# Windowed attention ahead of two MoE layers: q and k with one token to a partition, v's second copy made on the chip, zero fills moved, last output halves reordered

## The chip, the cores and the metric

The kernel runs on one core of one Trainium2 chip. The metric is the device time of one execution in microseconds; a table below gives the median of three runs and the one execution that was profiled. Engines are named as in the profile: PE is TensorE, PEld its weight loads, ACT is ScalarE, DVE is VectorE, POOL is GpSimd, SP is SyncE, which issues all transfers here.

## What is computed

An attention over 2 batches, 8 heads, 576 tokens and 64 columns a head, in which each query sees 32 keys: heads 0 to 3 the last 32 tokens, heads 4 to 7 every fourth token of the last 128. Its output, 1152 tokens by 512 columns, goes through a layer of 2048 columns with the Mish function and then through four experts of 1024 columns whose outputs are summed by probability.

```python
def _attn_ref(q, k, v):                      # q, k, v: [2, 8, 576, 64]
    scores = (1 / np.sqrt(D)) * np.matmul(q, k.transpose(0, 1, 3, 2))
    mask_plain = (rel >= 0) & (rel < 32)
    mask_dil = (rel >= 0) & (rel < 128) & (rel % 4 == 0)
    scores = np.where(masks, scores, -1e9)   # heads 0-3 plain, 4-7 dilated
    attn = np.exp(scores - max); attn = attn / (sum + 1e-09)
    return np.matmul(attn, v)

h = x @ w_in;  g = h * np.tanh(softplus(h));  x = g @ w_out
for e in range(4):
    out += p[:, e:e + 1] * (np.maximum(x @ w1[e], 0) @ w2[e])
```

`w_in` and `w_out` arrive as 64-bit floats.

## The kernel before

The program is scheduled by hand: each engine runs its instructions in the order of the source, and an engine waits where an operand of another engine or of a transfer is not there yet. Two accesses of one PSUM bank by different engines are put in order too.

**Attention units.** The attention is cut into ten units, five chunks of 128 tokens (the fifth of 64) for each of two batches (`Unit`, from L292). A unit's life is spread over several steps of `att_step` (L436). In step s the unit s+5 has its q and k loaded, s+2 is transposed on TensorE (`transposes`, L320), s+1 is copied from PSUM to SBUF on ScalarE (`spread`, L338), s has its scores (L344 to L355), its max, subtract and exp (`softmax`, L363 to L365) and the transposes of its probabilities (`probsT`, L377), s-1 has these copied (`probsT_copy`, L382) and multiplied by v (`values`, L389 and L393), its sums (L369) and its normalising (`normalise`, L401), and s-2 is transposed (`xT`, L409) and written as a high and a low part (`x_hi`, L420, ScalarE; `x_lo`, L424, VectorE).

**q and k.** A tile `nat` holds pairs of tokens: k on partitions 0 to 63 and q on 64 to 127, 128 columns (two tokens of one head) for each head, loaded in runs of 512 bytes, q and k each onto 64 partitions (L311). Eight transposes lead to PSUM, and eight ScalarE copies (L338) sort parity and head into `qkP` (heads 0 to 3) and `qkD` (heads 4 to 7), in which the two heads of a pair stand block by block in a matrix whose other blocks are zero. These zeros are written once by memsets (`zero_k`), for the first chunk on VectorE and for the rest on GpSimd.

**v.** `vP` and `vD` hold for each query block the keys of the block before (32 partitions) and its own (32 partitions), so that each token of v is there twice. Both copies are loaded from DRAM (L265, L269, L284, L288), in runs of 256 bytes for `vP` and of 1024 for `vD`. The zero blocks are GpSimd memsets at the start (`zero_v`).

**Weights.** `w_in` and `w_out` come as 32 blocks of 512 KiB onto 128 partitions into three buffers `raw` (`dec_load`, L131 and L134). Each is decoded over three steps: VectorE shifts (L150) and merges (L157), ScalarE makes a 16-bit rounding (L173) and the high part (L179), GpSimd the low part (L164). In the attention one block a step passes through; `dec_dve` stands at the end of a step, `dec_act` in its middle. Three blocks are loaded ahead, in steps -1, 0 and 1; after that each freed buffer is filled again.

**After the attention.** The first layer's multiplies (`first`, L497, and `second`, L517) begin in the last two steps of the attention; then follow the two layers' multiplies (L497, L517, L700, L753). At the end each tile of 128 rows of the output is multiplied by its probability on VectorE (`finish`, L767) and stored (L769); the last tile is cut into two halves of 256 columns that lie in one PSUM bank.

Of the kernel before, what the change touches and what calls it, by code (L numbers as in the profile page):

```python
# [8 lines left out]
F32 = mybir.dt.float32  # L9
# [14 lines left out]
def kernel(  # L24
# [177 lines left out]
    def zero_v(c):  # L202
        blk = slice(4 * c, min(4 * c + 4, S // 32))
        for j in range(2):
            POOL.memset(vP[64 * j:64 * j + 64, :, blk, 1 - j, :], 0.0)
            if c == 0:
                POOL.memset(vP[64 * j:64 * j + 32, :, 0, j, :], 0.0)
        if c in (0, NCH - 1):
            POOL.memset(vD[:, :, :, c], 0.0)
        else:  # L210
            for j in range(2):
                POOL.memset(vD[64 * j:64 * j + 64, :, 1 - j, c], 0.0)

    def zero_k(c, eng):
        n = min(128, S - 128 * c)
        for j in range(2):
            rows = slice(64 * j, 64 * j + 64)
            eng.memset(qkP[rows, :, 1 - j, 32 + 128 * c:32 + 128 * c + n], 0.0)
            eng.memset(qkD[rows, :, 1 - j, c + 1, :, 0:n // 2], 0.0)
# [15 lines left out]
    DVE.memset(qkP[:, :, 0:2, 0:32], 0.0)  # L235
    for p in range(2):
        DVE.memset(qkD[:, p, 0:2, 0], 0.0)
        DVE.memset(qkD[:, p, 0:2, NCH, :, (S % 128) // 2:64], 0.0)
    zero_k(0, DVE)
# [20 lines left out]
    def load_vP(b, g0, g1):  # L260

        for j in range(2):
            src = v[b, j:j + 1]
            if g0 == 0:
                SP.dma_start(out=vP[64 * j + 32:64 * j + 64, :, 0, j, :],  # L265
                             in_=bass.AP(src.tensor, src.offset, [[D, 32], [2 * S * D, 2], [1, D]]))
            g = max(g0, 1)
            for p in range(2):
                SP.dma_start(out=vP[64 * j:64 * j + 64, p, g:g1, j, :],  # L269
                             in_=bass.AP(src.tensor, src.offset + (2 * p * S + 32 * (g - 1)) * D,  # L270
                                         [[D, 64], [32 * D, g1 - g], [1, D]]))

    def load_vD(b, c0, c1):

        for j in range(2):
            src = v[b, 4 + j:5 + j]
            lo, n = 64 * j, 64
            off = src.offset + 128 * (c0 - 1) * D
            if c0 == 0:
                lo, n, off = lo + 32, 32, src.offset  # L280
            elif c1 == NCH:
                n = 32 + (S - 128 * c0) // 4
            if c1 == c0 + 1:
                SP.dma_start(out=vD[lo:lo + n, :, j, c0, :],  # L284
                             in_=bass.AP(src.tensor, off, [[4 * D, n], [2 * S * D, 2], [1, 4 * D]]))
                continue
            for p in range(2):
                SP.dma_start(out=vD[lo:lo + n, p, j, c0:c1, :],  # L288
                             in_=bass.AP(src.tensor, off + 2 * p * S * D,
                                         [[4 * D, n], [128 * D, c1 - c0], [1, 4 * D]]))  # L290


    v_loads = {-2: [(load_vD, 0, 1, NCH - 1)], -1: [(load_vP, 0, 8, S // 32), (load_vD, 0, NCH - 1, NCH)],
               2: [(load_vD, 1, 0, 1), (load_vP, 1, 0, 8)], 4: [(load_vD, 1, 1, NCH - 1)],
               5: [(load_vP, 1, 8, S // 32), (load_vD, 1, NCH - 1, NCH)]}

    class Unit:
# [8 lines left out]
        def load_qk(self):  # L306

            self.nat = ap1.tile([128, H, 2 * D], F32, tag="nat", name=nm("nat"), bufs=4)
            rows = slice(128 * self.c, 128 * self.c + self.n)
            for lo, src in ((0, k), (self.n // 2, q)):  # L310
                SP.dma_start(out=self.nat[lo:lo + self.n // 2],  # L311
                             in_=src[self.b, :, rows, :].rearrange("h (t two) d -> t h (two d)", two=2))

        def transposes(self):
            n = self.n
            self.pts = []
            for g in range(2):
                pt = bank(self.tbanks[g]).rearrange("p (h t) -> p h t", h=4)
                for h in range(4):
                    PE.transpose(pt[:, h, 0:n], self.nat[0:n, 4 * g + h, :], ident[0:n, 0:n])  # L320
                self.pts.append(pt[:, :, 0:n].rearrange("p (a j) (k t) -> p a j k t", j=2, k=2))

        def spread(self):

            n, c = self.n, self.c

            def move(g, par, j):
                src = slice(64 * par, 64 * par + 64)
                dst = slice(64 * j, 64 * j + 64)
                if g == 0:  # L330
                    cols = 32 + 128 * c
# [104 lines left out]
    def att_step(s, mid=None, pre=None):  # L436
# [3 lines left out]
        if n1:  # L440
            n1.spread()
# [473 lines left out]
```

## Time and profile before

| what | us |
|---|---|
| median of 3 runs | 666.11 (664.84 to 666.72) |
| the profiled execution | 663.83 |
| its span from the first to the last instruction | 662.1 |
| TensorE busy | 637.3 (96%) |
| VectorE, ScalarE, GpSimd busy | 290.9, 274.9, 158.4 |

The profile is of one execution. Busy time is the time in which an engine had an instruction under way; matmuls are pipelined and overlap. A row of the timeline gives the start in microseconds from the beginning of the span, the duration, the engine, the line of the kernel, the operation, out<-in by the program's names, the shape, and how many were merged into the row; in brackets stands how long the engine had been idle before it, and what ended that. PEclk is TensorE's granted clock as a share of full speed.

### The profile page before, as it was taken

To read this page: it belongs to the slowest core of one execution; us is meant where nothing else is said; L and a number is where in the kernel's file an instruction comes from. 1 tells how busy PE (TensorE), PEld (TensorE's weight loads), DVE (VectorE), ACT (ScalarE), POOL (GpSimd) and SP (SyncE) were. 2 spreads that over 40 slices of the span, in tenths; PEclk is the share of its full clock that TensorE was granted. 3 is DMA by queue.
4 is the path that set the end of the run, shared out by engine and by line. 5 is a ranking of instruction groups with operands and counts; after the bars stand their busy time and mean duration, and the time that the engine had idled before them with its cause. 6 is when DMAs were issued, how large, how long until landed. Compare 5 with 4: busy or idle time off the path is not lost.

```text
span 662.1 us, 10164 instructions
## 1 busy us (share of the span) xinstructions
PE 637.3 (96%) x4154; PEld 566.2 (86%) x4154; DVE 290.9 (44%) x491; ACT 274.9 (42%) x553; POOL 158.4 (24%) x170
## 2 busy tenths in 40 slices
PE   8687899999999999999999999999999999999997
PEld 5555678888999999988989899998899898899986
DVE  2567875661310234246443542544622534623323
ACT  6896676662422244444243412244322344322220
POOL 8011245551210023333034310043400143300000
PEclk9997999999999999999999999999999999999999
DMA  9999346640000023201022110022110032000102
GB/s 187 212 201 194 124 133 194 184 157 0 1 1 1 1 70 96 91 28 37 1 64 63 64 65 1 0 64 82 55 56 1 1 97 95 2 1 1 63 1 80
DMA packets 47454, 45.82 MB, mean 69 GB/s; under 512 B 12208, under 2 KB 40240, under 8 KB 47408
## 3 DMA queue, kind: packets, MB, share of 16 engines
q1 hardware_dynamic: 47408, 45.18, 25.4%
q8 instruction: 32, 0.52, 0.3%
q14 instruction: 14, 0.11, 0.1%
HBM read 42.81 MB, written 2.36 MB: 68 GB/s over the span
## 4 chain that ended last, share of the span: by engine, by line
PE 88%; ACT 4%; DMA 3%; DVE 2%; issue 1%; SPq 1%; ACTq 0%; DVEq 0%
PE bank L753 30%; PE bank L700 27%; PE bank L517 15%; PE bank L497 14%; DMA nat<-in_q_dram 2%; DMA raw<-in_moe_w_in_dram 1%; PE bank L320 1%; ACT qkD L338 1%; ACT qkP L338 1%; ACT xh L420 1%; ACT pT L382 0%; DVE scr L150 0%; DVE xl L424 0%; ACT pr L365 0%; PE bank L377 0%
## 5 line engine op out<-in xcount | busy, mean ns | idle before, releaser
L700 PE MATMUL bank<-xh,late 128*128 128x256 f32 (+1 forms) x512 | 120.7, 297 | 0.8 <-ACT late L712 0.7
L700 PE MATMUL bank<-wxh,late 128*128 128x320 f32 (+1 forms) x384 | 94.6, 296 | 0.0
L700 PEld LDWEIGHTS bank<-xh,late 128*128 128x128 f32 x512 | 88.3, 188 | 5.1 <-ACT late L712 2.2
L753 PE MATMUL bank<-late,gh 128*128 128x512 f32 x288 | 89.2, 391 | 0.0
L497 PE MATMUL bank<-xh,late 128*128 128x320 f32 (+1 forms) x288 | 76.6, 338 | 0.7 <-ACT scr L502 0.7
L700 PE MATMUL bank<-xl,late 128*128 128x256 f32 (+1 forms) x256 | 75.3, 294 | 0.0
L517 PE MATMUL bank<-gh,late 128*128 128x320 f32 (+1 forms) x288 | 72.6, 338 | 0.0
L700 PEld LDWEIGHTS bank<-wxh,late 128*128 128x128 f32 x384 | 67.8, 188 | 0.0
L656 POOL TENSOR_TENSOR raw<-raw 128x256 f32<-128x256 f32 x16 | 12.2, 764 | 228.4 <-DVE late L545 228.4
L506 DVE TENSOR_TENSOR gl<-scr,gh 128x512 fp32r<-128x512 f32 (+1 forms) x32 | 25.0, 780 | 84.3 <-ACT gh L505 84.3
L753 PEld LDWEIGHTS bank<-late,gh 128*128 128x128 f32 x288 | 52.3, 188 | 9.7
L502 ACT ACTIVATE scr<-bank 128x320 f32<-128x320 f32 (+1 forms) x48 | 23.4, 492 | 85.6 <-PE bank L497 85.6
L718 DVE TENSOR_TENSOR raw<-bank,late 128x256 f32<-128x256 f32 (+1 forms) x32 | 14.6, 457 | 100.7 <-PE bank L700 92.4
L753 PE MATMUL bank<-late,gl 128*128 128x512 f32 x144 | 56.7, 394 | 0.0
L700 PE MATMUL bank<-wxl,late 128*128 128x256 f32 (+1 forms) x192 | 56.3, 293 | 0.0
L544 ACT ACTIVATE late<-raw 128x512 fp32r<-128x512 f32 (+1 forms) x64 | 48.2, 782 | 17.1 <-PE bank L753 16.8
L497 PEld LDWEIGHTS bank<-xh,late 128*128 128x128 f32 x288 | 50.7, 188 | 5.3 <-ACT scr L502 1.0
L517 PEld LDWEIGHTS bank<-gh,late 128*128 128x128 f32 x288 | 50.1, 188 | 4.3
L545 POOL TENSOR_TENSOR late<-raw,late 128x1024 fp32r<-128x1024 f32 x16 | 38.7, 2417 | 61.4 <-ACT late L544 61.4
L753 PE MATMUL bank<-late,late 128*128 128x512 f32 (+1 forms) x219 | 52.8, 388 | 0.0
L700 PEld LDWEIGHTS bank<-xl,late 128*128 128x128 f32 x256 | 48.1, 188 | 2.5
L497 PE MATMUL bank<-xl,late 128*128 128x320 f32 (+1 forms) x144 | 48.6, 338 | 0.0
(140 smaller groups left out, 1171.1 us busy)
## 6 DMA issues: line engine op xcount, KB each, us to landing
raw<-in_moe_w_dram SPq DMA_DIRECT2D x32, 512.0 KB, 3.5
raw<-in_moe_w_in_dram SPq DMA_DIRECT2D x16, 512.0 KB, 4.0
raw<-in_moe_w_out_dram SPq DMA_DIRECT2D x16, 512.0 KB, 3.5
nat<-in_k_dram SPq DMA_DIRECT2D x8, 256.0 KB, 5.4
nat<-in_q_dram SPq DMA_DIRECT2D x8, 256.0 KB, 5.8
out_dram<-scr SPq DMA_DIRECT2D x8, 256.0 KB, 2.1
vD<-in_v_dram SPq DMA_DIRECT2D x8, 192.0 KB, 7.2
vP<-in_v_dram SPq DMA_DIRECT2D x8, 160.0 KB, 7.7
```

Of the source, the lines that this page charges most:

```text
L320: PE.transpose(pt[:, h, 0:n], self.nat[0:n, 4 * g + h, :], ident[0:n, 0:n])
L338: ACT.activation(*move(g, par, j), AF.Copy)
L497: PE.matmul(h, a[:, c, :], x[:, c, :], start=c == 0 and k == 0, stop=c == 3 and k == 2)
L502: ACT.activation(self.hc[:, self.w * i:self.w * (i + 1)], h, AF.Mish)
L506: DVE.tensor_tensor(out=self.glo, in0=self.hc, in1=self.ghi.bitcast(F32), op=ALU.subtract)
L517: PE.matmul(yacc[self.grp][d], a[:, s], x[:, g], start=u == UORD[self.grp][0] and k == 0, stop=u == UORD[self.grp][-1] and k == 2)
L544: ACT.activation(hi, src, AF.Copy)
L545: eng.tensor_tensor(out=lo, in0=src, in1=hi.bitcast(F32), op=ALU.subtract)
L656: POOL.tensor_tensor(out=a22, in0=a21, in1=a22, op=ALU.add)
L700: PE.matmul(out, w, x(k), start=first and k == 0 and i == 0, stop=k == 1 and i == 2, skip_group_check=not first)
L718: DVE.tensor_tensor(out=self.cb[:, 0:N], in0=self.c, in1=p1, op=ALU.add)
L753: PE.matmul(acc, x[:, s], a[:, cols], start=self.p == 0 and f == 0 and i == 0, stop=self.p == NP2 - 1 and f == 1 and i == 2, skip_group_ch ...
```

## The change

q and k are loaded into two tiles, one token to a partition, in runs of 256 bytes onto up to 128 partitions. Four transposes each bring two heads at a time; three ScalarE copies per unit go to `kk` (two copies, with zero blocks as before) and `qq` (one). The dilated heads' scores read every fourth column of `kk` and `qq`. The zero blocks of `kk` are written by VectorE at the start. v is loaded once, into each block's own 32 partitions, and GpSimd copies it from there to the 32 partitions of the block before (`copy_v`), in the step before the unit's scores. `zero_v` of chunks 0 and 1 stays at the start; those of chunks 2 to 4 go into steps 0, 1 and 2. The loads of v stand in steps -2, 2, 4 and 5, the first three loads of weights in steps 0, 1 and 2. In a step the sums now stand ahead of `values` and the normalising ahead of `x_hi` and `x_lo`. At the end the multiply by the probability and the store of the last tile's two halves come behind both halves' matmuls.

```diff
-    qkP = ap1.tile([128, 2, 3, 32 + S], F32, name="qkP")
-    qkD = ap1.tile([128, 2, 3, NCH + 1, 2, 64], F32, name="qkD")
+    kk = ap1.tile([128, 4, 2, 128 * (NCH + 1)], F32, name="kk")
+    qq = ap1.tile([128, 4, S], F32, name="qq")
...
+    def zero_k(c):
         for j in range(2):
+            DVE.memset(kk[64 * j:64 * j + 64, :, 1 - j, 128 * c + 128:128 * c + 256], 0.0)
...
+    for j in range(2):
+        DVE.memset(kk[:, :, j, 0:128], 0.0)
+        DVE.memset(kk[:, 2:4, j, 128 + S:], 0.0)
+    for j in range(2):
+        DVE.memset(vD[64 * j + 32:64 * j + 64, :, j, NCH - 1], 0.0)
+    for c in range(NCH):
+        zero_k(c)
     zero_v(0)
-    for c in range(1, NCH):
-        zero_k(c, POOL)
-        zero_v(c)
     for t in raws:
         POOL.memset(t[:, 4096:4104].bitcast(U32), 0)
+    zero_v(1)
...
+    def load_v(b, c0, c1):
+        g0, g1 = 4 * c0, min(4 * c1, S // 32)
+        cf = min(c1, S // 128)
         for j in range(2):
+            own = slice(64 * j + 32, 64 * j + 64)
             for p in range(2):
+                src = v[b, 2 * p + j:2 * p + j + 1]
+                SP.dma_start(out=vP[own, p, g0:g1, j, :],
+                             in_=bass.AP(src.tensor, src.offset + 32 * g0 * D, [[D, 32], [32 * D, g1 - g0], [1, D]]))
...
+    def copy_v(c):
+        g0, g1 = max(4 * c, 1), min(4 * c + 4, S // 32)
         for j in range(2):
+            before, own = slice(64 * j, 64 * j + 32), slice(64 * j + 32, 64 * j + 64)
+            POOL.tensor_copy(vP[before, :, g0:g1, j, :], vP[own, :, g0 - 1:g1 - 1, j, :])
+            if c:
+                POOL.tensor_copy(vD[before, :, j, c, :], vD[own, :, j, c - 1, :])
+    v_loads = {-2: (0, 2, NCH), 2: (1, 0, 2), 4: (1, 2, 4), 5: (1, 4, NCH)}
...
         def load_qk(self):
-            self.nat = ap1.tile([128, H, 2 * D], F32, tag="nat", name=nm("nat"), bufs=4)
             rows = slice(128 * self.c, 128 * self.c + self.n)
-            for lo, src in ((0, k), (self.n // 2, q)):
-                SP.dma_start(out=self.nat[lo:lo + self.n // 2],
-                             in_=src[self.b, :, rows, :].rearrange("h (t two) d -> t h (two d)", two=2))
+            self.nat = []
+            for x in "kq":
+                t = ap1.tile([128, H, D], F32, tag="nat" + x, name=nm("nat" + x), bufs=4)
+                SP.dma_start(out=t[0:self.n], in_=(k if x == "k" else q)[self.b, :, rows, :].rearrange("h t d -> t h d"))
+                self.nat.append(t.rearrange("p h d -> p (h d)"))
...
         def spread(self):
-            for g in range(2):
-                for par in range(2):
-                    for j in range(2):
-                        ACT.activation(*move(g, par, j), AF.Copy)
+            n, t0 = self.n, 128 * self.c
+            for j in range(2):
+                rows = slice(64 * j, 64 * j + 64)
+                ACT.activation(kk[rows, :, j, 128 + t0:128 + t0 + n], self.pt[0][rows], AF.Copy)
+            ACT.activation(qq[:, :, t0:t0 + n], self.pt[1], AF.Copy)
...
                 for r in range(4):
                     PE.matmul(s[32 * r:32 * r + n // 4, 256 + 128 * p:384 + 128 * p],
-                              qkD[:, p, 2, c + 1, r % 2, r // 2:n // 2:2],
-                              qkD[:, p, 0:2, c:c + 2, r % 2, r // 2::2], start=False, stop=True, skip_group_check=True)
+                              qq[:, 2 + p, t0 + r:t0 + n:4], kk[:, 2 + p, :, t0 + r:t0 + 256:4],
+                              start=False, stop=True, skip_group_check=True)
...
         if p1:
             p1.probsT_copy()
+        if n1:
+            copy_v(n1.c)
+        if 0 <= s < NCH - 2:
+            zero_v(s + 2)
         if n1:
             n1.spread()
...
         if p1:
+            p1.sums()
             p1.values()
         if p2:
             p2.xT()
         if p1:
-            p1.sums()
+            p1.normalise()
         if p2:
             p2.x_hi()
             p2.x_lo()
         if DEC0 <= s < NA:
             dec_act()
-        if p1:
-            p1.normalise()
...
-        if DEC0 - 4 <= s < DEC0 - 1:
+        if DEC0 - 3 <= s < DEC0:
             dec_load()
...
     for t in range(len(accs)):
         for f in range(2):
             g.second(f, slice(t, t + 1))
-        g.finish(slice(t, t + 1))
+        if t < len(accs) - 2:
+            g.finish(slice(t, t + 1))
+    g.finish(slice(len(accs) - 2, len(accs)))
```

## Rows read from the trace of the kernel before

**Rows 1.** Busy time by stretches: stretch, length, busy us of each engine (instructions), PEclk, DMA share, GB/s

```profile
50.00:60.00 10.00, 6.20 (x85) 4.74 (x84) 6.94 (x15) 5.83 (x15) 1.29 (x1) 0.83 1.13 199
90.00:100.00 10.00, 10.00 (x46) 8.16 (x45) 6.93 (x10) 6.94 (x13) 4.99 (x4) 1.00 0.67 194
```

**Rows 2.** The chain that ended last, in order of time: start, us, what

```profile
25.64 6.22 DMA nat<-in_q_dram
...
48.72 8.69 DMA raw<-in_moe_w_in_dram
...
85.83 2.60 PE bank L517 x10
```

**Rows 3.** Timeline of ScalarE from 14 to 90 us

```profile
16.20 0.60 ACT L382 ACTIVATE pT<-bank 128x512 f32<-128x512 f32 x1 [1.38 <-PE bank L377]
...
33.60 0.60 ACT L382 ACTIVATE pT<-bank 128x512 f32<-128x512 f32 x1 [0.46 <-PE bank L377]
...
40.31 1.67 ACT L338 ACTIVATE qkP<-bank 64x256 f32<-64x256 f32 x4
42.01 1.54 ACT L338 ACTIVATE qkD<-bank 64x256 f32<-64x256 f32 x4
...
62.38 0.60 ACT L382 ACTIVATE pT<-bank 128x512 f32<-128x512 f32 x1
```

**Rows 4.** Timeline of VectorE from 11 to 90 us

```profile
50.27 0.43 DVE L150 TENSOR_SCALAR scr<-raw 128x512 uint32<-128x512 uint32 x1 [3.48 <-DMA raw<-in_moe_w_out_dram]
...
57.50 0.43 DVE L150 TENSOR_SCALAR scr<-raw 128x512 uint32<-128x512 uint32 x1 [2.37 <-DMA raw<-in_moe_w_in_dram]
...
61.48 0.98 DVE L424 TENSOR_TENSOR xl<-bank,xh 128x256 fp32r<-128x256 f32 x2 [0.59 <-ACT xh L420]
...
62.95 1.21 DVE L150 TENSOR_SCALAR scr<-raw 128x512 uint32<-128x512 uint32 x1
...
69.18 1.27 DVE L150 TENSOR_SCALAR scr<-raw 128x512 uint32<-128x512 uint32 x1
```

**Rows 5.** Timeline of TensorE from 14 to 90 us

```profile
21.52 0.64 PE L351 MATMUL bank<-qkP 128*32 128x128 f32 x16
21.99 0.64 PE L355 MATMUL bank<-qkD 128*32 128x128 f32 x16
...
68.28 0.60 PE L377 MATMUL bank<-ident,pr 128*128 128x128 f32 x4
...
74.27 0.60 PE L377 MATMUL bank<-ident,pr 128*128 128x128 f32 x4
```

**Rows 6.** Busy time by stretches of 1 us, columns as in rows 1

```profile
7.00:8.00 1.00, 0.83 (x4) 0.43 (x3) 0.00 (x0) 0.96 (x3) 0.92 (x3) 1.00 1.20 220
21.00:22.00 1.00, 1.00 (x23) 0.60 (x24) 0.00 (x0) 0.63 (x2) 0.00 (x0) 1.00 1.36 164
...
56.00:57.00 1.00, 1.00 (x26) 1.00 (x20) 0.00 (x0) 0.95 (x4) 0.32 (x1) 0.50 1.37 179
61.00:62.00 1.00, 1.00 (x16) 0.61 (x17) 0.52 (x2) 1.00 (x3) 0.00 (x0) 0.77 0.97 384
```

**Rows 7.** Timeline of the transfers' issue on SyncE

```profile
11.62 0.63 SPq L311 DMA_DIRECT2D nat<-in_q_dram  x1
...
59.85 0.53 SPq L793 DMA_DIRECT2D prob<-in_moe_domain_probs_dram  x1
```

**Rows 8.** Timeline of VectorE at the start, and of GpSimd

```profile
2.31 0.27 DVE L218 MEMSET qkP<- 64x256 f32 x1
...
14.13 1.07 POOL L212 MEMSET vD<- 64x512 f32 x2
...
62.57 1.30 POOL L164 TENSOR_TENSOR wxl<-scr,wxh 128x512 fp32r<-128x512 f32 x1 [6.25 <-ACT wxh L179]
```

**Rows 9.** Timeline of the last 7 us, VectorE and TensorE

```profile
656.46 1.20 DVE L767 SCALAR_TENSOR_TENSOR scr<-bank,prob,scr 128x512 f32<-128x512 f32 x2 [0.64 <-PE bank L753]
...
657.72 0.50 PE L753 MATMUL bank<-late,wxh 128*128 128x256 f32 x2 [0.58 <-DVE scr L767]
```

More of the change, by code (lines that the diff above doesn't have):

```diff
@@ L234 @@
         DVE.memset(t, 0.0)
[L235 to L239, printed above, removed]
+    for j in range(2):
[5 more added lines that the diff above has]
+        zero_k(c)
     zero_v(0)
-    for c in range(1, NCH):
-        zero_k(c, POOL)
-        zero_v(c)
     for t in raws:
         POOL.memset(t[:, 4096:4104].bitcast(U32), 0)
+    zero_v(1)
     for g in range(4):
@@ L273, in load_vD @@
-    def load_vD(b, c0, c1):
-        for j in range(2):
[L276 to L290, printed above, removed]
@@ new lines, in load_v @@
+            src = v[b, 4 + j:5 + j]
+            for p in range(2 if cf > c0 else 0):
+                SP.dma_start(out=vD[own, p, j, c0:cf, :],
+                             in_=bass.AP(src.tensor, src.offset + (2 * p * S + 128 * c0) * D,
+                                         [[4 * D, 32], [128 * D, cf - c0], [1, 4 * D]]))
+            if cf < c1:
+                n = (S - 128 * cf) // 4
+                SP.dma_start(out=vD[64 * j + 32:64 * j + 32 + n, :, j, cf, :],
+                             in_=bass.AP(src.tensor, src.offset + 128 * cf * D, [[4 * D, n], [2 * S * D, 2], [1, 4 * D]]))
@@ L314, in transposes @@
         def transposes(self):
             n = self.n
-            self.pts = []
-            for g in range(2):
[L318 to L321, printed above, removed]
-        def spread(self):
[L325 to L331, printed above, removed]
-                    return qkP[dst, :, j:3:2 - j, cols + par:cols + n:2], self.pts[0][src, :, j]
-                return qkD[dst, :, j:3:2 - j, c + 1, par, 0:n // 2], self.pts[1][src, :, j]
-            for g in range(2):
-                for par in range(2):
-                    for j in range(2):
-                        ACT.activation(*move(g, par, j), AF.Copy)
+            self.pt = []
@@ new lines, in transposes @@
+            for x, nat in enumerate(self.nat):
+                pt = bank(self.tbanks[x]).rearrange("p (a t) -> p a t", a=4)[:, :, 0:n]
+                for a in range(4):
+                    PE.transpose(pt[:, a], nat[0:n, 128 * a:128 * a + 128], ident[0:n, 0:n])
+                self.pt.append(pt)
+        def spread(self):
+            n, t0 = self.n, 128 * self.c
[3 more added lines that the diff above has]
+            ACT.activation(qq[:, :, t0:t0 + n], self.pt[1], AF.Copy)
@@ L429 @@
         au[n].load_qk()
[L430 to L431 removed]
+    load_v(0, 0, 2)
     def unit_at(n):
@@ L468, in att_step @@
             unit_at(s + 5).load_qk()
-        for load, *args in v_loads.get(s, ()):
-            load(*args)
-        if DEC0 - 4 <= s < DEC0 - 1:
+        if s in v_loads:
+            load_v(*v_loads[s])
+        if DEC0 - 3 <= s < DEC0:
             dec_load()
@@ L798 @@
     u1.probsT_copy()
+    u1.sums()
     u1.values()
@@ L801 @@
     steps[0].act()
-    u1.sums()
     dec_act()
```

36 lines of the change are left out of this document (8 added, 28 removed).

## Prediction, made before the changed kernel was run

> **What bounds the kernel.** I read first the busy time by stretches: from 90 us on TensorE is busy 10.00 of 10 us, but from 50 to 60 us only 6.20, while the DMA share there is 1.13 [rows 1]. Then the chain of work that ended last: its unbroken run of matmuls begins at 85.83 us, and ahead of it stand waits for two transfers, a q tile (6.22 us) and a weight block (8.69 us) [rows 2]. So only what happens before 85.83 us, and the last tile, can move the time; the multiplies between them are not touched.
>
> Inside the front I use two landmarks. The copy of the transposed probabilities, ScalarE L382, starts one step: units 0, 3 and 7 at 16.20, 33.60 and 62.38 us [rows 3]. VectorE's L150, the first operation of the weight decoding, closes a step: 50.27, 57.50, 62.95 and 69.18 us [rows 4]. The first two of these wait for weight blocks, 3.48 and 2.37 us: there the queue of transfers sets the pace. From 62.95 to 69.18, 6.23 us, no transfer is waited for; VectorE works nearly without a break and waits 0.59 us for ScalarE's `xh` in such a step [rows 4]. From 68.28 to 74.27 us TensorE is the pace, 5.99 us for a step with a MoE multiply in it [rows 5].
>
> **Transfers.** Up to the fifth weight block, for which L150 waited until 57.50 us, the old order moves 4608 KiB of q and k, 3584 of v (1600 in 256-byte runs, 1984 in 1-KiB runs) and 2560 of weights. The new order drops the second copy of v and has, ahead of the same block, 4608, 2176 (half and half) and 2560. Rates by [rows 6]: 512-byte runs onto 64 partitions 220 GB/s; 256-byte runs onto 64 partitions 164 and 179, so 172; weight blocks onto 128 partitions 384. The new v runs go onto 32 partitions; I keep 172 and 220 for them. Before: 21.4 + 9.5 + 9.2 + 6.8 = 47.0 us. The queue started at about 2.5 us and the block landed at 57.41 [rows 2], 54.9 us, a factor of 1.17 with its gaps, which I keep. New are q and k in 256-byte runs onto 128 partitions, which no row shows. By the run length they would go at 172 GB/s, 27.4 us; by the partitions at 384, 12.3 us. Neither row is nearer, since each shares one property, so I take the middle in time, 20.0 us (236 GB/s). Then 20.0 + 6.5 + 5.1 + 6.8 = 38.4, times 1.17, plus 2.5 = 47.3 us for the fifth block, 10 us earlier; by the ends 38.3 and 56.0. The issue itself took 0.63 us for a q load of 512 runs and 0.53 for the 1152 of `prob` [rows 7], so I charge nothing for the 1024 of a new load; at twice 0.63 the twenty loads would cost SP 13 us more, and what covers that is the backlog of transfers ahead of them.
>
> [...]
>
> **ScalarE.** A unit's spreading is eight copies, 1.67 and 1.54 us [rows 3], 3.2 in all. Three copies of 512 columns take its place; by L382's 0.60 us for 128x512 [rows 3] that is 1.5 (starts overlapped) to 1.8 us; I take 1.8, so 1.4 us less a unit. In steps without decoding that is on the path, because the exp stands behind it: pT 0.5, spread 3.2, exp 0.6 and the transposes of the probabilities 0.7 make some 5.2 us; with 1.8 it would be 3.6. TensorE's own work then ends later: mask and scores 1.3, values 1.1 (by the 16 matmuls of L351 and L355, 0.47 us from start to start), and three sets of transposes (0.60 for four, so 0.6, 0.9 and 0.6 with overlaps) [rows 5] make 4.4 us, 3.8 in the step that has fewer. Until unit 0 TensorE runs through, so there I take 0.5 us for q and k that land earlier: unit 0 at 15.7, unit 3 at 15.7 + 3.8 + 4.4 + 4.4 = 28.3 instead of 33.60, in which a transfer was waited for [rows 2]. The new order's load of unit 5 has 2816 KiB of q and k and 1152 of v up to it, by the rates and factor above at 24 us, and is needed at about 27.
>
> **VectorE.** Normalising now stands ahead of `x_lo` and fills the 0.59 us of waiting: 6.23 - 0.6 = 5.64 us a decode step. It needs the values of one unit and `xT` of the one before, which TensorE issues right behind the scores (1.8 us, against 2.4 of max, subtract and sums on VectorE), so its wait costs nothing; queued behind it are `x_lo` and L150, and TensorE's next `xT` would wait. The fills put on VectorE are 16 memsets, 14 of them of 512 columns; 256 columns took 0.27 us [rows 8], so 7.8 us, until about 9.2 us. The first max is due at 11 to 12 us: a cover of 2 us, and a shortfall would be paid in full.
>
> **GpSimd.** It gets 4 copies of 32x512 a unit. No row has a copy on GpSimd. From below: it must at least write, and a memset of 512 columns took 0.53 us (1.07 for two); from above: a two-input operation of 128x512 took 1.30 [rows 8]. One input is nearer to the memset; I take 0.75 us, 3.0 a unit. The first v lands at about 13.5 us (1536 KiB of q and k, 512 of v). Between that and unit 4's multiply by v stand 17 such copies and 12 fills, 5.9 us: 13.5 + 12.8 + 5.9 = 32.2 us, against unit 4's step at about 33. That is barely covered, and TensorE's whole queue stands behind it. The other cost is collision: L150 took 1.21 us beside the GpSimd operation that began at 62.57 [rows 8], and 0.43 without one [rows 4]. With a copy queued behind that operation, the next VectorE operation between SBUF tiles can wait 0 to 0.75 us more in each decode step; I take 0.45. So 6.1 us a step, between 5.6 and 6.5.
>
> **The rest.** Weight blocks start loading one step later, but behind fewer bytes; by the same sum the first lands at about 25.5 us and is wanted at 25: a wait of some 0.5 us on VectorE, which lies within the bounds of the landmark below. The dilated scores stride by 4 elements instead of 2 on both operands. Stride 2 cost as stride 1 did, 0.64 us for 16 in both [rows 5]; from nothing to as much again, 0.47 us a unit, and on the path only in the last two steps: 0 to 1 us, taken at 0. The tail: the last half's matmuls waited 0.58 us for the first half's multiply by `prob` [rows 9]; that goes, but the first half's multiply (0.45 of the pair's 1.20) then most likely stands behind the last matmuls, ahead of the last multiply, and its store goes out just before the last one: 0, within 0.3 us.
>
> **Sum.** The decode step that follows unit 3's copy ends with L150 about 0.9 us behind it, at 29.2 us (28 to 31). Four decode steps of 6.1 lead to 53.6, where the old kernel had 62.95: 9.3 us. The fifth weight block is there (47.3 against 47.5). From that point both kernels have two steps on TensorE's or VectorE's pace and the same run-out to the unbroken matmuls, 22.9 us. [...] So 663.83 - 9.3 = 654.5 us for the profiled execution. That execution is 2.3 us (0.3%) under the median of the runs shown, 666.11; on the median I get 656.8, say 657.
>
> **Rivals.** (a) The 256-byte runs go at 172 GB/s whatever the partitions: the fifth block lands at 56.0 instead of 57.4, the transfers keep the pace, and 0 to 3 us are gained by shorter steps behind it; about -2.5 us, 663.6. For it: two rows at 164 and 179. Against it: 384 only on 128 partitions. [...] (b) GpSimd's copies cost 1.3 us: unit 4's v is ready at 13.5 + 22.1 + 5.9 = 41.5, unit 5 starts at 44, the steps after it take 4 x 1.3 + 1.3 = 6.5 us, and unit 7 comes at 57 instead of 62.38: -5.4 us, 660.7. (c) Slower: GpSimd paces the whole front. With c us a copy unit 7 comes at 13.5 + 5.9 + 17c + 2.5 + 2(4c + 1.3), which passes 62.38 from c = 1.52 us on; at 1.8 us the time is 7.1 us longer, 673.2. For it: the copies shift partitions, which no row prices. Against it: one input is less than the two that took 1.30. (d) The front gets shorter but the run-out eats it, because it takes a weight block a step and L150 again meets blocks that are not there: within 2 us of now. Against it: from 61 to 62 us the queue moved 384 GB/s, a block in 1.4 us, and there is no backlog behind the fifth.
>
> **Chances.** Forecast 0.5 (its own range 654 to 660), (a) 0.17, (b) 0.13, (c) 0.09, (d) 0.11. What a measurement of this kernel can tell from no change is about 0.3%, 2 us; most of (a) lies beyond it. Faster: 0.5 + 0.13 + most of (a) = 0.78; same 0.12; slower 0.10. The low end is steps of 5.6 us and the fast end of the transfers, -12.5 us: 653.5; the high end takes in (a) and (b), 663.8. Left out are (c) and most of (d).
>
> **What would show it.** In the changed profile: L382's counterpart for unit 3 near 28 and for unit 7 near 53 us; q and k moving at well over 172 GB/s; no wait of L150 for weight blocks; GpSimd copies near 0.75 us; VectorE without a wait ahead of `x_lo`; the unbroken matmuls from about 76.5 us; the last two output multiplies back to back. Wrong would be: TensorE waiting for GpSimd ahead of the multiply by v, L150 still waiting for transfers, or decode steps over 6.5 us.

## The result, and the profile after

The changed kernel takes 657.39 us (median of 4 runs, 656.95 to 657.64); the kernel before took 666.22 on the same chip (4 runs). The ratio is 0.987, 95% interval 0.9853 to 0.9887: 8.8 us less. The forecast was 657.0. The profiled execution took 657.5 us, its span is 655.7; before's was 662.1.

So the medians differ by 8.8 us but the two profiled executions by 6.4: before's was 2.4 us under its median, after's at its own. Where the time went is read from the traces, so from the 6.4.

The chain of waits of after, in order of time (start, us, what). Ahead of the matmuls stand three transfers, again a q tile and a weight block as in [rows 2], but shorter:

```profile
2.73 4.85 DMA natq<-in_q_dram
...
18.86 3.78 DMA natq<-in_q_dram
...
35.27 4.78 DMA raw<-in_moe_w_in_dram
```

ScalarE's copy of the transposed probabilities, L363 now, for units 0, 3 and 7; in [rows 3] they stood at 16.20, 33.60 and 62.38:

```profile
13.55 0.60 ACT L363 ACTIVATE pT<-bank 128x512 f32<-128x512 f32 x1 [1.08 <-PE bank L358]
...
31.03 0.60 ACT L363 ACTIVATE pT<-bank 128x512 f32<-128x512 f32 x1
...
56.92 0.60 ACT L363 ACTIVATE pT<-bank 128x512 f32<-128x512 f32 x1
```

VectorE, with the first, third, fifth, sixth and eighth weight block at L150; the fourth to seventh of before stood at 50.27, 57.50, 62.95 and 69.18 in [rows 4]:

```profile
7.98 2.38 DVE L213 MEMSET kk<- 64x512 f32 x4
10.39 0.69 DVE L344 TENSOR_REDUCE mx<-bank 128x8 f32<-128x512 f32 x1
...
26.45 0.56 DVE L150 TENSOR_SCALAR scr<-raw 128x512 uint32<-128x512 uint32 x1 [3.30 <-DMA raw<-in_moe_w_in_dram]
...
40.14 0.74 DVE L150 TENSOR_SCALAR scr<-raw 128x512 uint32<-128x512 uint32 x1 [3.10 <-POOL vP L280]
...
51.23 0.43 DVE L150 TENSOR_SCALAR scr<-raw 128x512 uint32<-128x512 uint32 x1
...
57.15 0.43 DVE L150 TENSOR_SCALAR scr<-raw 128x512 uint32<-128x512 uint32 x1
57.49 1.80 DVE L157 SCALAR_TENSOR_TENSOR scr<-raw,scr 128x512 uint32<-128x512 uint32 x1
...
69.28 0.42 DVE L150 TENSOR_SCALAR scr<-raw 128x512 uint32<-128x512 uint32 x1
```

The wait at 40.14 is put down to a GpSimd copy, but the chain shows what ended last: the third weight block, issued at 35.27 and landed at 40.05. VectorE's fills run into the first max at 10.39 with no gap: the cover of 2 us that the prediction gave them is used up.

TensorE: the plain and the dilated scores of a unit (L332, L336), the wait for the q tile of unit 4, the same scores behind it, and the first of the unbroken matmuls, which stood at 85.83 in [rows 2]:

```profile
17.32 0.65 PE L332 MATMUL bank<-kk,qq 128*32 128x128 f32 x16
17.79 1.10 PE L336 MATMUL bank<-kk,qq 128*32 128x128 f32 x16
...
22.78 0.66 PE L310 MATMUL bank<-ident,natq 64*128 64x64 f32 x4 [1.19 <-DMA natq<-in_q_dram]
...
24.94 1.08 PE L332 MATMUL bank<-kk,qq 128*32 128x128 f32 x16
...
80.19 0.50 PE L501 MATMUL bank<-gl,wxh 128*128 128x512 f32 x1 [0.46 <-DVE gl L490]
```

GpSimd's copies of v and the low part of a block (L164):

```profile
14.13 0.61 POOL L280 COPY vP<-vP 32x512 f32<-32x512 f32 x1
...
57.17 1.56 POOL L164 TENSOR_TENSOR wxl<-scr,wxh 128x512 fp32r<-128x512 f32 x1 [1.31 <-DMA prob<-in_moe_domain_probs_dram]
58.80 0.73 POOL L280 COPY vP<-vP 32x256 f32<-32x256 f32 x1
```

Busy time by stretches, columns as in [rows 1]: the new q and k loads run at 217 GB/s from 7 to 8 us; from 17 to 18 us the queue moves 21 GB/s; from 22 to 30 us TensorE's clock is granted at 0.57 on average and at 0.50 from 23 to 29, after it had waited 0.81 us for `pr` and 1.19 for the q tile; from 55 to 60 us VectorE is busy 4.79 of 5 us:

```profile
7.00:8.00 1.00, 0.45 (x4) 0.38 (x4) 0.71 (x3) 0.99 (x3) 0.97 (x2) 1.00 1.39 217
17.00:18.00 1.00, 1.00 (x23) 0.71 (x25) 0.00 (x0) 0.83 (x2) 0.94 (x3) 1.00 0.17 21
22.00:30.00 8.00, 7.22 (x82) 5.57 (x83) 4.38 (x10) 2.60 (x7) 6.21 (x13) 0.57 1.22 276
55.00:60.00 5.00, 4.89 (x80) 3.52 (x79) 4.79 (x10) 3.53 (x9) 3.62 (x5) 1.00 0.30 55
```

**The one table that sorts all executions.** For each profiled execution: when VectorE's L150 takes the fifth weight block, how long from there to the eighth, how long from the eighth to the unbroken matmuls, and the rest of the span. The lower rows are the experiments below.

| kernel | 5th block, us | 5th to 8th | run-out | rest | span | median (of the kernel before beside it) |
|---|---|---|---|---|---|---|
| before | 57.50 | 17.85 | 10.48 | 576.27 | 662.1 | 666.22 |
| before, again | 59.94 | 17.75 | 11.80 | 576.11 | 665.6 | one run, 667.41 |
| after | 51.23 | 18.05 | 10.91 | 575.51 | 655.7 | 657.39 (666.22) |
| `v_twice` | 58.27 | 18.15 | 10.88 | 575.80 | 663.1 | 664.63 (665.96) |
| `qk_pairs` | 51.83 | 18.39 | 10.85 | 575.73 | 656.8 | 659.20 (665.96) |
| `old_order` | 52.28 | 18.91 | 11.85 | 575.86 | 658.9 | 660.08 (665.96) |
| `old_tail` | 52.55 | 17.68 | 12.19 | 576.28 | 658.7 | 658.96 (665.96) |
| `raw_first` | 49.86 | 17.83 | 12.18 | 575.33 | 655.2 | 656.96 (666.58) |
| `qk4_first` | 49.31 | 17.55 | 10.92 | 575.32 | 653.1 | 656.03 (666.58) |
| `raw_early` | 52.74 | 17.85 | 12.22 | 575.59 | 658.4 | 657.62 (665.29) |
| `dense` | 50.54 | 18.11 | 10.89 | 575.36 | 654.9 | 656.40 (666.58) |
| `copies_twice` | 50.29 | 17.74 | 11.29 | 575.28 | 654.6 | 658.48 (666.58) |
| `lo_late` | 51.87 | 18.10 | 10.90 | 575.93 | 656.8 | 659.29 (667.32) |
| `both` | 50.02 | 18.01 | 10.89 | 575.98 | 654.9 | 657.43 (667.32) |

Behind the fifth block before takes 17.85 + 10.48 + 576.27 = 604.6 us and after 604.5; 6.27 of the 6.4 us lie ahead of it. The run-out is 10.5 to 10.9 us in eight executions, in which the transposes of `xn` behind its wait (L390 in after, L409 in before) take 0.66 us, and 11.8 to 12.2 in the five in which they take 1.12 (before again, `old_order`, `old_tail`, `raw_first`, `raw_early`); `copies_twice` has 11.29 with 0.66 and a clock of 1.00. TensorE's clock was granted at 1.00 throughout the run-out in before and after, and at 0.86 on average in before again, `raw_first` and `raw_early` (an estimate from stretches of 5 us, of which the lowest have 0.77, 0.66 and 0.75).

A row is one execution and can lie off its kernel's median: `raw_early`'s took 2.6 us more, `old_tail`'s 1.5 more, `copies_twice`'s 1.8 less, `qk4_first`'s 1.2 less. `old_tail` has the same front as after and takes the fifth block 1.32 us later, so a difference of that size in that column shows nothing about an edit.

### The profile page after: what moved, and what is told of

It reads as the page before. It is cut to its first block, busy times and chain, and to the rows that moved or that the text cites. A ratio compares the mean times of both kernels' runs of the same rounds, so it can differ in the third digit from the quotient of the medians.

```text
span 655.7 us, 10182 instructions
## 1 busy us (share of the span) xinstructions
PE 638.3 (97%) x4154; PEld 566.7 (86%) x4154; DVE 296.8 (45%) x498; ACT 261.3 (40%) x503; POOL 177.7 (27%) x194
## 4 chain that ended last, share of the span: by engine, by line
PE 91%; DVE 3%; DMA 2%; ACT 2%; SPq 1%; issue 1%; POOL 0%; DVEq 0%; ACTq 0%
PE bank L737 30%; PE bank L684 27%; PE bank L501 15%; PE bank L481 14%; DMA natq<-in_q_dram 1%; PE bank L336 1%; PE bank L310 1%; DMA raw<-in_moe_w_in_dram 1%; PE bank L332 1%; PE bank L358 1%; DVE scr L157 1%; PE bank L390 1%; PE bank L370 0%; DVE xl L405 0%; DVE pr L345 0%
## 5 line engine op out<-in xcount | busy, mean ns | idle before, releaser
L640 POOL TENSOR_TENSOR raw<-raw 128x256 f32<-128x256 f32 x16 | 12.2, 765 | 228.7 <-DVE late L529 228.7
```

Of the source, the lines that this page charges most:

```text
L640: POOL.tensor_tensor(out=a22, in0=a21, in1=a22, op=ALU.add)
```

## Experiments

**One part undone at a time.** `v_twice` loads both copies of v from DRAM again and drops the copies on GpSimd:

```diff
-        if n1:
-            copy_v(n1.c)
...
-        if s in v_loads:
-            load_v(*v_loads[s])
+        for load, *args in v_loads.get(s, ()):
+            load(*args)
```

> The changed kernel with v loaded twice from DRAM as before (its loads where they stood before) and no copies on GpSimd; all else as changed. My theory, that the second copy of v kept the queue of transfers full: most of the gain goes, 6 to 8 of the 8.8 us, so 663 to 666 us, and L150 waits for weight blocks again for 4 to 6 us in sum. Rival, that the gain comes from ScalarE's and VectorE's shorter steps: 657 to 660 us. Rival, that GpSimd's copies hold the front up: under 657 us.

Measured: 664.63 us (12 runs), ratio to before 0.9968 (0.9948 to 0.9988): 7.2 of the gain are gone. VectorE's L150 waits for the first, third and fifth block, 13.2 us in sum, where 4 to 6 were expected:

```profile
31.36 0.43 DVE L150 TENSOR_SCALAR scr<-raw 128x512 uint32<-128x512 uint32 x1 [6.59 <-DMA raw<-in_moe_w_in_dram]
...
44.70 0.43 DVE L150 TENSOR_SCALAR scr<-raw 128x512 uint32<-128x512 uint32 x1 [2.78 <-DMA raw<-in_moe_w_in_dram]
...
58.27 0.43 DVE L150 TENSOR_SCALAR scr<-raw 128x512 uint32<-128x512 uint32 x1 [3.86 <-DMA raw<-in_moe_w_in_dram]
```

The second copy of v is 1408 KiB up to that block; by the prediction's rates and factor that is (9.5 + 9.2 - 6.5 - 5.1) x 1.17 = 8.3 us, and the fifth block came 7.0 us later. So the second copy of v carries most of the gain. The kernel also has the old order of v's loads and no copies on GpSimd, so its 7.2 us are not the bytes' alone.

`qk_pairs` puts the old layout of q and k back (pairs of tokens, eight copies on ScalarE), with v still copied:

```diff
-            for x in "kq":
-                t = ap1.tile([128, H, D], F32, tag="nat" + x, name=nm("nat" + x), bufs=4)
+            self.nat = ap1.tile([128, H, 2 * D], F32, tag="nat", name=nm("nat"), bufs=4)
```

> The changed kernel with q and k in pairs of tokens as before (512-byte runs onto 64 partitions, eight copies on ScalarE a unit, dilated scores with stride 2, their zero fills all on VectorE); v, order and tail as changed. My theory (transfers first): q and k move at the same rate either way (220 GB/s in the changed trace, 220 before), so only ScalarE's 1.4 us a unit comes back in the early steps, against which stands 0.46 us a unit less on TensorE: 658 to 661 us. Rival (ScalarE's spreading is what was won): 663 to 666 us. Rival (stride 4 and 256-byte runs cost more than the copies saved): 655 to 657 us.

Measured: 659.20 us, ratio 0.9898 (0.987 to 0.9926), 1.8 us over after. That is no more than what the two intervals leave open. The fifth block is taken at 51.83 against 51.23, so no effect of the layout on the transfers shows; that what it gives is ScalarE's shorter spreading is argued, and no row here shows it.

`old_order` puts the sums behind `values` and the normalising behind `x_lo`, as before:

```diff
-            p1.sums()
             p1.values()
...
-            p1.normalise()
```

> The changed kernel with the sums behind the multiply by v and the normalising behind x_lo, as before. My step: VectorE waits 0.6 us for xh again in each of the decode steps that VectorE paces; by the changed trace these are the steps from 51 to 69 us, three of them: +1.5 to +2 us, 659 us. Rival (the weight merge L157 or another VectorE operation just meets the GpSimd operation elsewhere, so the wait is only moved): within 0.5 us of 657.4.

Measured: 660.08 us, ratio 0.99 (0.9873 to 0.9928), 2.7 over after. VectorE waits for ScalarE's `xh` again, 0.31 to 0.45 us in each of the last steps:

```profile
57.21 1.03 DVE L405 TENSOR_TENSOR xl<-bank,xh 128x256 fp32r<-128x256 f32 x2 [0.31 <-ACT xh L401]
...
63.57 0.98 DVE L405 TENSOR_TENSOR xl<-bank,xh 128x256 fp32r<-128x256 f32 x2 [0.45 <-ACT xh L401]
```

In the table 0.86 us of it lie between the fifth and the eighth block, where it is the slowest of all. The 1.05 ahead of the fifth is less than what `old_tail` with an unchanged front differs by, and the 0.94 in the run-out comes with L390 at 1.12 us in it, as where the lower clock was measured. So 0.9 us is shown for the order of VectorE's work, and not 2.7.

`old_tail` multiplies each half of the last tile right behind its own matmuls, as before:

```diff
-        if t < len(accs) - 2:
-            g.finish(slice(t, t + 1))
-    g.finish(slice(len(accs) - 2, len(accs)))
+        g.finish(slice(t, t + 1))
```

> The changed kernel with the last two halves finished one after the other, as before. By my prediction 0, within 0.3 us; by the changed trace, in which the last multiply ends 1.4 us after the last tile's first half began to be multiplied and the span behind the last full tile is shorter by some 0.7 us: +0.7 us, 658.1.

Measured: 658.96 us, ratio 0.9895 (0.9866 to 0.9924). The median alone can't tell 0.7 from nothing, but the rest of the span can: 576.1 to 576.3 in the three executions with the old tail, 575.3 to 576.0 in the eleven with the new, 0.6 us less on average. The last multiply waits 1.07 us for its own matmuls here, which had waited for the first half's multiply as in [rows 9]; in after the pair takes 0.87 us with both halves' matmuls behind it:

```profile
653.32 1.20 DVE L751 SCALAR_TENSOR_TENSOR scr<-bank,prob,scr 128x512 f32<-128x512 f32 x2 [0.64 <-PE bank L737]
655.59 0.48 DVE L751 SCALAR_TENSOR_TENSOR scr<-bank,prob,scr 128x256 f32<-128x256 f32 x1 [1.07 <-PE bank L737]
```

And after:

```profile
652.14 0.87 DVE L751 SCALAR_TENSOR_TENSOR scr<-bank,prob,scr 128x256 f32<-128x256 f32 x2 [0.68 <-PE bank L737]
```

**The order of the transfers.** The parts undone sum to 13.3 us, more than the 8.8 gained. That would fit parts that share one limit, but each ratio's interval is 1.3 to 2 us to either side, and the moved zero fills were not undone by themselves. Three kernels move loads on SyncE's queue and leave the bytes as they are. `raw_first`:

```diff
-        if s in v_loads:
-            load_v(*v_loads[s])
         if DEC0 - 3 <= s < DEC0:
             dec_load()
+        if s in v_loads:
+            load_v(*v_loads[s])
```

> The changed kernel with the weight load ahead of the loads of v within a step (nothing is left out). Theory (the issue order on SyncE still costs the front): in the changed kernel the third weight block was issued at 35.27 us behind eight v loads and landed at 40.05, L150 waited 3.10 us for it, and TensorE's clock stood at 0.50 right after it. With the block issued first, at about 28 us, that wait goes and the steps behind it lie 2 to 3 us earlier: about 655 us against 657.4, and L150 without a wait of over 1 us between 36 and 42 us. Rival (the wait is only moved): the v loads of the second batch, some 2 us later, are then late for GpSimd's copies, or the next q and k, and the time stays within 1 us of 657.4.

Measured: 656.96 us, ratio 0.9854 (0.9826 to 0.9883). The third block is there, but VectorE now waits for the fifth; the median is 0.4 under after's, so the rival's outcome. In its profiled execution the fifth block is taken 1.4 us earlier than in after, and the run-out, with the clock granted at 0.66 from 70 to 75 us, is 1.3 us longer:

```profile
49.86 0.73 DVE L150 TENSOR_SCALAR scr<-raw 128x512 uint32<-128x512 uint32 x1 [1.79 <-DMA raw<-in_moe_w_in_dram]
```

`qk4_first` moves ten loads of v behind k and q of unit 4 as well:

```diff
-    v_loads = {-2: (0, 2, NCH), 2: (1, 0, 2), 4: (1, 2, 4), 5: (1, 4, NCH)}
+    v_loads = {-1: (0, 2, NCH), 2: (1, 0, 2), 4: (1, 2, 4), 5: (1, 4, NCH)}
```

> raw_first, and besides the ten loads of v's rest of batch 0 one step later, behind k and q of unit 4 (nothing is left out). Theory (issue order): unit 3's and unit 4's q and k no longer stand behind those ten loads (issued 18.06 to 18.86 us in the changed kernel, a q tile on the chain of waits for 3.78 us), unit 3's pT L363 comes near 28 us as in the prediction instead of 31.03, TensorE isn't left standing before 23 us, so its clock isn't at 0.50 from 23 to 30 us, and another 2 to 3 us go: 652 to 654 us. Rival: v then lands too late for the copies of units 2 to 4, TensorE's multiply by v waits for GpSimd, and the time is that of raw_first or up to 3 us longer.

Measured: 656.03 us, ratio 0.9853 (0.9823 to 0.9884), the lowest median of all, though its interval reaches after's. The wait for the q tile is gone, but unit 3's copy still comes at 31.01: L150 waits for the first weight block, unit 3's max stands behind it on VectorE, and TensorE stands 2.68 us.

```profile
27.38 0.43 DVE L150 TENSOR_SCALAR scr<-raw 128x512 uint32<-128x512 uint32 x1 [3.04 <-DMA raw<-in_moe_w_in_dram]
27.73 0.68 DVE L344 TENSOR_REDUCE mx<-bank 128x8 f32<-128x512 f32 x1
```

The row of TensorE that waits for it:

```profile
29.85 0.69 PE L358 MATMUL bank<-ident,pr 128*128 128x128 f32 x4 [2.68 <-ACT pr L346]
```

The fifth block, waited for 1.05 us and taken at 49.31, was issued only behind eight loads of v, which SyncE issued from 39.46 to 45.12 us. From 43.5 to 46.5 us the queue moved 134 and 126 GB/s in two stretches of 1.5 us, against up to 336 earlier, so it was not full:

```profile
44.11 1.01 SPq L267 DMA_DIRECT2D vD<-in_v_dram  x2
45.21 0.39 SPq L131 DMA_DIRECT2D raw<-in_moe_w_in_dram  x1
```

`raw_early` loads the first three blocks a step earlier on top of that, as the kernel before did:

```diff
-        if DEC0 - 3 <= s < DEC0:
+        if DEC0 - 4 <= s < DEC0 - 1:
```

> qk4_first with the first three weight blocks loaded in steps -1, 0 and 1, as in the kernel before, instead of 0, 1 and 2 (nothing is left out). In qk4_first the first block is issued at 20.98 us and lands at 27.29, L150 waits 3.04 us for it with the next unit's max queued behind. Theory (the change put the loads a step too late): issued near 13.7 us, the block is there when L150 is due at 24.4, the wait goes, and the steps behind it lie 2 to 3 us earlier: 653 to 654 us against 656.0. Rival (the bytes set the pace): the queue has as many bytes to move up to the fifth block as in qk4_first, so what the first block gains v or q and k lose (waits for natk, natq or v of units 2 to 4), L150 waits as long for a later block, and by the step at which VectorE's steps of 6 us begin (49.3 us in qk4_first) the two are within 1 us: 655.5 to 656.5.

Measured: 657.62 us, ratio 0.9869 (0.9839 to 0.99). The wait for the first block is gone and unit 3's copy comes at 29.00, near the forecast's 28.3; in its place VectorE waits 1.43 us for the second block, 5.60 for the fourth and 1.27 for the fifth:

```profile
46.40 0.43 DVE L150 TENSOR_SCALAR scr<-raw 128x512 uint32<-128x512 uint32 x1 [5.60 <-DMA raw<-in_moe_w_out_dram]
...
52.74 0.73 DVE L150 TENSOR_SCALAR scr<-raw 128x512 uint32<-128x512 uint32 x1 [1.27 <-DMA raw<-in_moe_w_in_dram]
```

The median fits neither expectation, and the fifth block, for which the rival had both kernels within 1 us, is taken 3.4 us later than in `qk4_first`. In all three the order of loads decides which block is waited for. The fifth is taken between 49.31 and 52.74 us, and none of the medians differs from after's by more than the intervals.

**What lies beside it.** `dense` lets the dilated scores read neighbouring columns; heads 4 to 7 then score other keys than the reference's.

```diff
-                              qq[:, 2 + p, t0 + r:t0 + n:4], kk[:, 2 + p, :, t0 + r:t0 + 256:4],
+                              qq[:, 2 + p, t0 + r:t0 + r + n // 4], kk[:, 2 + p, :, t0 + r:t0 + r + 64],
```

> The changed kernel with the dilated heads' scores reading neighbouring columns instead of every fourth one; heads 4 to 7 then score other keys than the reference's. It prices the stride alone. In the changed kernel's trace the 16 dilated matmuls took 1.10 us a unit against 0.64 for those of stride 1, 0.46 us more, which the prediction took as 0 (0 to 1 us in all). If the stride is the cause, the group takes 0.64 us here; if TensorE paces the front in most steps, up to ten units' 0.46 us come back, twice that at half clock: 3 to 5 us, 652 to 654. If it paces only in the last two steps, as the prediction has it, 1 us or less: 656.4 to 657.4. In between I take 655.5.

Measured: 656.40 us, ratio 0.9858 (0.9829 to 0.9887). The group falls from 1.10 to 0.62 us, so the stride costs 0.48 us a unit at a granted clock of 1.00. At 0.50 after shows 1.13 us (L336 at 25.80) beside 1.08 for the plain scores, so 0.05 there, and not the double that was expected. The group in `dense`:

```profile
17.45 0.62 PE L336 MATMUL bank<-kk,qq 128*32 128x128 f32 x16
```

But from the fifth to the eighth block it is 18.11 us with 0.48 us a step less on TensorE where its clock is at 1.00 (from 55 to 60 us it was granted at 0.66), against 18.05: behind the fifth block VectorE waits for nothing there, so TensorE isn't the pace. The 1.0 us of the median lies inside the intervals, so no gain is shown.

`copies_twice` makes each of GpSimd's copies twice, 1.2 us instead of 0.60:

```diff
-            POOL.tensor_copy(vP[before, :, g0:g1, j, :], vP[own, :, g0 - 1:g1 - 1, j, :])
+            for _ in range(2):
+                POOL.tensor_copy(vP[before, :, g0:g1, j, :], vP[own, :, g0 - 1:g1 - 1, j, :])
...
```

> The changed kernel with each of GpSimd's copies of v made twice, so that one token's copy costs 1.2 us instead of 0.60 (nothing is left out). It gives rival (b) of the prediction its price. By its working unit 4's v is ready some 17 x 0.6 = 10 us later than in the changed kernel, the multiply by v waits for GpSimd, and unit 7 comes some 3 to 4 us later: 660.5 us, with TensorE's waits for vP and vD at L370 and L374 in the trace. Other theory (in the changed kernel the transfers and not GpSimd pace units 1 to 5, and GpSimd stands idle enough in these steps): within 1 us of 657.4.

Measured: 658.48 us, ratio 0.9879 (0.9853 to 0.9905), 1.1 over after, and the profiled span is 1.1 us shorter than after's. GpSimd is then busy 4.86 to 4.89 of 5 us from 30, 40 and 50 us on; TensorE's multiply by v (L371) waits for it 0.73 us in unit 0, as long as it stood there in after, and in no other unit. VectorE's L150 waits 0.61 and 0.39 us for L164. The stretch from 40 us:

```profile
40.00:45.00 5.00, 2.68 (x29) 1.81 (x33) 4.79 (x12) 3.36 (x7) 4.89 (x7) 0.74 1.15 219
```

So rival (b)'s price was too high: 0 to 1 us, not 3 to 4, where the multiply by v of unit 4 comes at 37 us in after, not at the 33 it was forecast for.

`lo_late` puts GpSimd's L164 behind the copies of the next step:

```diff
-            POOL.tensor_tensor(out=units[u][1][:, s], in0=kwbuf[(n - 2) % 3].bitcast(F32),
-                               in1=units[u][0][:, s].bitcast(F32), op=ALU.subtract)
+            lows.append((units[u][1][:, c], kwbuf[(n - 2) % 3].bitcast(F32), units[u][0][:, c].bitcast(F32)))
...
         if 0 <= s < NCH - 2:
             zero_v(s + 2)
+        dec_low()
```

> The changed kernel with GpSimd's low part of a weight block (L164) put behind the next step's copies of v instead of ahead of them (nothing is left out). In the changed kernel L157 on VectorE took 1.80 us in three steps in which L164 had begun just before it (57.17, 63.26 us), against 0.68 elsewhere, and the steps from 51.23 to 69.28 us are 5.92, 6.09 and 6.04 us with VectorE busy 4.8 of 5 us. Theory (VectorE paces these steps and pays the meeting in full): L157 falls to about 0.7 us in them, the steps come to 5.0 to 5.6 us, and 2 to 3 us go: 654.9 us, 654.3 to 655.6. Rival (TensorE, busy nearly throughout in the same stretch, holds the step at 6 us): L157 falls but VectorE then waits for TensorE, and the time stays at 656.5 to 657.5. Other rival (the meeting moves to the next operation between SBUF tiles, the sums L350): no gain either, with L350 over 1 us.

Measured: 659.29 us, ratio 0.9879 (0.9853 to 0.9904): no gain. It doesn't answer its question. GpSimd is so far ahead with its copies that L164 starts right behind them (58.01 us) or as soon as ScalarE's high part is there (63.82 and 69.96), and meets L157, in one step L150, all the same:

```profile
58.13 1.78 DVE L157 SCALAR_TENSOR_TENSOR scr<-raw,scr 128x512 uint32<-128x512 uint32 x1
```

`both` is `qk4_first` with that edit.

> qk4_first with L164 put behind the next step's copies, as in lo_late (nothing is left out). If issue order and VectorE's meeting with L164 are separate costs, the gains add: 656.0 less 2 to 3, 653 to 654 us. If the wait for weight blocks is the limit as soon as the steps get shorter (the queue of transfers moved 206 to 240 GB/s in most of the front), L150 waits again and the time is that of qk4_first, 655.5 to 656.5.

Measured: 657.43 us, ratio 0.9855 (0.9829 to 0.9881): as `qk4_first`, with 1.74 us of waiting for the fifth block. What the meeting costs in the whole was not settled: no kernel here is rid of it.

`before_again` is the kernel before in a second profiled execution.

> The kernel before once more, for a second profile of it (nothing is changed). Its profiled execution, on which the prediction rests, took 663.83 us and lay 2.3 us under the median. If executions differ by how long TensorE runs at half clock in the front, this one has other stretches of PEclk below 1.00 than 50 to 65 us, L150's 75.35 us and the unbroken matmuls' 85.83 us lie later by what its time is above 663.83, and its run-out from that L150 is 10.5 us, or some 11.8 where the half clock falls into it.

Measured: 667.41 us. The fifth block is 2.44 us later than in the first execution, and the run-out 1.32 us longer, with TensorE's clock granted at 0.77 from 80 to 85 us and the multiply by v in it takes 0.85 us where the first execution has 0.52. The unbroken matmuls begin 3.66 us later, at 89.49, and the time is 3.58 us longer. The longer run-out with the lower clock in it was expected and found. It is 1.32 us of the difference; the other 2.34, by which the eighth block is later, lie ahead of it, where the first block is waited for 2.50 us against 0.94, and what delayed them stays open.

```profile
79.20 0.85 PE L389 MATMUL bank<-vP,pT 128*32 128x128 f32 x6 [2.48 <-ACT pT L382]
```

## Why the prediction was right, and where its steps were off

**The time is right, the sum behind it less so.** It was 654.5 us for the profiled execution and 2.3 more for the median. After's profiled execution took 657.5, 3.0 more than 654.5, and stands at its median. That 657 came so near 657.39 is luck in good part: the 3.0 us that the sum had too little were nearly made good by before's profiled execution lying 2.4 us under its median while after's did not. The base was one execution, which the rows of before all share, and `before_again` took 3.58 us more. Of the forecast's 9.3 us the pair of traces shows 5.64 at the unbroken matmuls (85.83 to 80.19) and 0.76 in the tail.

**What bounds it** was right in the main: transfers first (in after up to the third block, the last one waited for), then steps in which VectorE is nearly always busy, then a remainder that did not change. The steps from 51.23 to 69.28 us are 5.92, 6.09 and 6.04; the forecast was 6.1. From the sixth block to the unbroken matmuls it put 22.9 us and the trace has 23.04.

**The term that was mis-sized: the front up to the fifth block.** The sum took the sixth L150 at 53.6 and it is at 57.15, 3.55 later. 2.3 of it come by the second block (31.49 against 29.2), 1.26 in the four steps behind it.
- *Units 1 to 3* took 17.48 us from unit 0's copy to unit 3's; the forecast had 12.6. Unit 0 itself was 2.15 us earlier than forecast. The missing piece is the issue on SyncE, charged at nothing because a backlog would cover it. Between 17 and 20 us there was none: k and q of unit 4 stood behind ten loads of v, the queue moved 21 to 105 GB/s, and TensorE then waited 1.19 us for the q tile. From 23 to 29 us its clock was granted at 0.50, and L332 took 1.08 us instead of 0.65. With that wait alone gone (`qk4_first`) units 1 to 3 take 17.11 us; with the first block's gone as well (`raw_early`) they take 15.34, and TensorE still waits 2.15 us for q and k tiles.
- *The first block* was forecast to be waited for 0.5 us and was waited for 3.30; *the third* was not thought of, and was waited for 3.10 behind eight loads of v.
- *The rate of q and k* was taken at 236 GB/s and measured at 217 to 220, so by the same formula (21.6 + 6.5 + 5.1 + 6.8) x 1.17 + 2.5 = 49.3 us for the fifth block instead of 47.3. Kernels with v loaded once in which L150 waits for that block by more than 1 us take it at 49.86, 49.31 and 50.02 us (`raw_first`, `qk4_first`, `both`) and at 52.74 and 52.55 (`raw_early`, `old_tail`).
- *The gaps.* The 49.3 is no limit set by the bytes: at the measured rates they take 40.0 us, and the factor of 1.17 carries over the gaps of before. In after SyncE issues one load behind another from 0.74 to 47.36 us, also where the queue moves 21 GB/s (17 to 18 us); the 34 loads of v ahead of the fifth block take it 21.8 us, waits within them included, against (6.5 + 5.1) x 1.17 = 13.6 in the sum. In the five kernels named the block was issued right behind eight loads of v, and L150 could take it 4 to 5 us later. So the issue of v's small loads, again charged at nothing, may set when the fifth block comes, and with it why moving loads about brings so little. No run takes these loads out of its way or makes them fewer, so this is argued and not shown.

The price of 172 GB/s that rival (a) put on 256-byte runs does not hold: the 217 to 220 GB/s measured in after for 256-byte runs onto 128 partitions is under the 384 of weight blocks, over the 164 and 179 of 256-byte runs onto 64, and the same as 512-byte runs onto 64 partitions [rows 6]. Rival (a) fell with that. (c) needed copies of over 1.52 us, and they took 0.60; (d) needed a longer run-out with L150 waiting for blocks in it, and it is 10.91 us against 10.48, with no such wait.

**The smaller terms.** ScalarE's three copies take 1.8 us as forecast. GpSimd's copy takes 0.60 us, not 0.75, and holds nobody up. The meeting of GpSimd and VectorE was put at 0.45 us a step more than before and is 0.34, but by another cause: not copies queued behind L164 but L164 itself, which now meets L157 (1.80 us, 0.68 alone) instead of L150 (1.21, 0.43 alone); the copy at 58.80 waits, not VectorE. In after L164 runs from 57.17 to 58.73 us, and L157, begun at 57.49, ends at 59.29. At 45.44 L164 began ahead of L157 too, and there L164 took 2.21 us and L157 0.67; what decides between the two no run here shows. The order of VectorE's work, forecast at 0.6 us a step, gives 0.3 (0.86 in the three steps of `old_order`). The dilated stride, taken at 0, costs 0.48 us a unit at a clock of 1.00, but in steps that TensorE doesn't pace, so 0 on the path was near. The tail gives 0.6 us, where 0 within 0.3 was forecast: the two multiplies behind one wait take 0.87 us, while the old order paid a wait of 1.07 between them.

**Of the signs named ahead,** these came: q and k well over 172 GB/s, copies at 0.60 us, no wait ahead of `x_lo` in the decode steps of 6 us, the last two multiplies back to back. These didn't: unit 3 near 28 and unit 7 near 53 us (31.03 and 56.92), no wait of L150 for weight blocks (6.4 us in two, which the prediction named as a sign of being wrong), the unbroken matmuls from 76.5 (80.19).

## What to carry to other kernels

Where transfers set the pace, count the bytes that stand ahead of the transfer that is waited for, divide by rates seen in the trace, and count the time of the issue beside it: here the second copy of v carried most of the gain (7.2 of 8.8 us were gone with it back), but the 34 small loads that were left took SyncE 21.8 us, and each wait cut out by reordering came back at another block (1.79 us for the fifth in `raw_first`, 5.60 for the fourth in `raw_early`). Take the base of a sum from more than one execution: here the second one moved it by over 3 us, and the same front took the fifth block 1.3 us apart in two kernels.

## What the runs showed of the hardware that was not expected

- Scores that read every fourth fp32 column of both operands took 1.10 us for 16 matmuls against 0.62 with neighbouring columns, at a granted clock of 1.00; at 0.50 the two groups of after took 1.13 and 1.08. Every second column had cost nothing (0.64 us for both groups in [rows 5]).
- A GpSimd copy that shifts 32x512 fp32 by 32 partitions takes 0.60 us, 0.55 from start to start.
- SyncE issued a pair of 64-KiB loads of v in 0.79 us at the least, mostly in 0.9 or more; ten loads of v, 640 KiB, took it from 11.81 to 17.96 us, which is 106 GB/s (an estimate from their sizes and these rows). From 17 to 20 us the queue moved 21 to 105 GB/s, and TensorE then waited 1.19 us for the q tile that stood behind.
- TensorE's clock was granted at 0.50 behind some of its waits: in after behind 1.19 us at 22.78 and 3.67 us at 43.52, but at 1.00 behind 2.25 us at 71.21. Single matmul groups then took up to 1.7 times as long (L358 1.11 us at 23.36, 0.65 at 16.42), and where that fell into the run-out (five of fourteen executions, by the 1.12 us of the transposes of `xn` against 0.66), the run-out was some 1.3 us longer.
